# The second MLP's contraction by seven products of quarters, with products added onto each other in PSUM

## The chip, the core and the metric

The kernel runs on one core of a Trainium2 chip. The metric is the device time of one execution in microseconds; the time given is the median of three runs. One more execution was profiled, and all rows come from that one.

## What is computed

Three parts run one after the other on 4 x 576 = 2,304 tokens with 512 features: attention with a banded mask, an MLP with a product gate, and an MLP with a Silu gate. The change lies in the last one, cut here to what matters:

```python
# x: (2304, 512), from attention and the first MLP
g = x @ w_gate                        # (2304, 1536)
silu = g * (1.0 / (1.0 + np.exp(-g)))
val = x @ w_val                       # (2304, 1536)
out = (silu * val) @ w_out            # (2304, 512)
```

## The kernel before

**Precision.** Every fp32 operand is split into two parts of the type fp32r, a rounded one (ScalarE, a copy) and the rest (VectorE, a subtraction): `to_parts`, lines 163 to 165. A product of two operands is three matmuls, `mm3`, lines 222 to 224. Its time appears at these three lines whatever is multiplied, so the names of the tiles tell the parts of the kernel apart.

**Stage 1** has attention and the first MLP, in chunks of 512 tokens and a last one of 256. For each of 8 groups of features, the gates `ba` (copied by ScalarE, line 241, to `ta`) and `bb` (multiplied by VectorE, line 247) are made, and the result is contracted. Beside it `quarters` prepares the weights of stage 2, one step at a time (`step`, called after each group; `work` is the list of steps): a block of 1 MB is loaded into one of two `raw` buffers, turned to fp32 (line 205 on ScalarE, 206 and 207 on VectorE), for the gate and value weights summed (lines 535 to 538), split by `split_to` (line 518 on ScalarE, 519 on GpSimd) and stored to the DRAM tensors `wd` and `wod` (line 556). `QUARTERS` says how many of the 18 blocks each chunk takes.

**Stage 2** runs over 3 column blocks `c` of 768 tokens and in each over 6 groups `j` of 256 features: 18 groups. The gate and the value of a group are each made by seven products of quarters (two halves of the 512 inputs, of the 256 features, of the 768 tokens), with sums and differences of quarters, in place of eight. `operands` makes the seven token-side sums once for a column block (line 629, split at 164 and 165); the weight-side ones come from `wd` through a ring of 14 places (`fill`, line 653), each of which holds the gate's and the value's part for one product. `product` makes product `r` for the gate and then for the value: 12 matmuls of 384 columns, each in its own PSUM bank of a set of three. `evacuate` reads the banks: a ScalarE copy for the first product (line 713), VectorE sums for the rest (line 704), Silu on ScalarE (707), the multiplication on VectorE (708), and the split of the result to `p`.

The contraction of a group with `w_out` is then plain: six units (`units`), one for 128 tokens, each 6 matmuls of 512 columns into one of two banks, and an addition to `acc` by VectorE (line 746; line 744 is a copy for the first group). Units go to the list `todo`, and `contract_some` takes one after each of the first six products of the next group. After the last group the remaining six run on their own. `load_wo` (line 760) loads two tiles of weights for a group, into four buffers.

The queues of the engines are filled by a scheduler that works on a model of the times, so an instruction of a later group may stand ahead of one of an earlier.

Of the kernel before, what the change touches and what calls it, by code (L numbers as in the profile page):

```python
# [10 lines left out]
F32 = mybir.dt.float32  # L11
# [65 lines left out]
S1, S2, S4, S3, A11, A12, A22 = range(7)  # L77
SPOT = [A11, S2, A12, S1, S3, S4, A22]

BANK = [0, 1, 2, 0, 1, 2, 0]  # L80

NOP = 9
NRING = 14

UNITS = [1, 1, 1, 1, 1, 1, 0]
# [4 lines left out]
def moe_chain_kernel(tc, q_in, k_in, v_in, w_in, mask_in, out):  # L90
# [8 lines left out]
    with static as st, other as ot, psum as pp, dram as dp:  # L99
# [16 lines left out]
        wd = dp.tile([FP, P, 7, 2, 2, 2 * P], F32R, name="wd")  # L116
        wod = dp.tile([FP, P, 2, 2 * 512], F32R, name="wod")
# [101 lines left out]
        def mm3(ps, w, x, start, stop):  # L219

            (wh, wl), (xh, xl) = w, x
            nc.tensor.matmul(ps, wh, xh, start=start, stop=False)  # L222
            nc.tensor.matmul(ps, wh, xl, start=False, stop=False)  # L223
            nc.tensor.matmul(ps, wl, xh, start=False, stop=stop)  # L224
# [52 lines left out]
        with att1_pool as a1, att2_pool as a2:  # L277
# [243 lines left out]
            def quarters():  # L521
# [7 lines left out]
                if kind != "wo2":  # L529

                    b = x.rearrange("p i (j f) -> p i j f", j=2)
                    t = raw_at[n][:, :, :, 1].bitcast(F32).rearrange("p i (j f) -> p i j f", j=2)
                    t = {S1: t[:, 0, 0], S2: t[:, 0, 1], S4: t[:, 1, 0], S3: t[:, 1, 1]}
                    add = nc.vector.tensor_tensor
                    add(out=t[S1], in0=b[:, 1, 0], in1=b[:, 1, 1], op=ALU.add)
                    add(out=t[S3], in0=b[:, 0, 0], in1=b[:, 1, 0], op=ALU.subtract)
                    add(out=t[S2], in0=t[S1], in1=b[:, 0, 0], op=ALU.subtract)
                    add(out=t[S4], in0=b[:, 0, 1], in1=t[S2], op=ALU.subtract)
                    yield
                for i in range(2):  # L540
                    stage = stages[n_stage[0] % 2]
                    n_stage[0] += 1
                    if kind == "wo2":
                        w = stage[:, :1024].rearrange("p (b h f) -> p b h f", b=1, h=2)
                        split_to(w, x[:, i:i + 1])
                        dst, src = wod[j, :, i], stage[:, :1024]
                    else:
                        w = stage.rearrange("p (s h f) -> p s h f", s=7, h=2)
                        m = ("wg", "wv").index(kind)
                        f = slice(i * P, (i + 1) * P)  # L550
# [45 lines left out]
        with mid_pool as mp:  # L596
# [19 lines left out]
            def operand(c, r):  # L616
                return ops[(7 * c + r) % NOP]
# [234 lines left out]
```

## Time and profile before

| | us |
|---|---|
| median of 3 runs (lowest, highest) | 877.03 (876.01, 877.11) |
| the profiled execution | 877.38 |
| its span | 875.6 |
| TensorE busy | 848.3 (97%) |
| VectorE busy | 563.3 (64%) |
| ScalarE busy | 347.4 (40%) |
| GpSimd busy | 110.3 (13%) |

In the rows PE is TensorE's matmuls, PEld its weight loads, DVE VectorE, ACT ScalarE, POOL GpSimd, SP SyncE, and a q behind an engine its queue. `out<-in` names tiles by the program's names. Matmuls overlap and their ends are modelled, so the time of one is read from the start of one to the start of the next. A busy time is the time in which at least one instruction ran.

### The profile page before, as it was taken

What the parts mean: (1) busy time and instruction counts of PE and PEld (TensorE: products, weight loads), DVE (VectorE), ACT (ScalarE), POOL (GpSimd) and SP (SyncE); (2) the same over time, 40 slices, a digit from 0 to 9 for tenths busy, and PEclk for the clock granted to TensorE, in tenths of its full rate; (3) what the DMA queues carried; (4) which work ended last, traced back from release to release, by engine and by line L of the source; (5) the groups of instructions that cost most, each with busy time, mean ns of one, the idle gap of its engine ahead of it and who ended that gap; (6) DMA issues with size and microseconds to landing.
All of it is one profiled execution on the core that took longest, in us unless ns stands there. A gap on an engine that the chain in (4) does not pass through costs nothing.

```text
span 875.6 us, 12949 instructions
## 1 busy us (share of the span) xinstructions
PE 848.3 (97%) x4846; PEld 744.6 (85%) x4846; DVE 563.3 (64%) x989; ACT 347.4 (40%) x819; POOL 110.3 (13%) x120
## 2 busy tenths in 40 slices
PE   7889999999999999999799999999999999999998
PEld 5668788888887777787799999999999999999997
DVE  6899964275437452363468766797666686666676
ACT  5687755375536453343344222242222232222221
POOL 1000144035304440153210000000000000000000
PEclk9889999999999999999899999999999999999999
DMA  9997558269625762785899666587766667766311
GB/s 294 345 286 260 179 167 277 53 189 318 215 69 172 255 186 84 235 267 189 267 360 389 204 210 214 179 285 233 244 201 197 205 215 258 226 214 215 122 49 72
DMA packets 79279, 188.20 MB, mean 215 GB/s; under 512 B 6896, under 2 KB 42352, under 8 KB 74480
## 3 DMA queue, kind: packets, MB, share of 16 engines
q1 hardware_dynamic: 76336, 182.65, 64.5%
q10 hardware_dynamic: 2880, 4.72, 1.5%
q8 instruction: 38, 0.62, 0.3%
q14 instruction: 25, 0.20, 0.1%
HBM read 148.29 MB, written 39.06 MB: 214 GB/s over the span
## 4 chain that ended last, share of the span: by engine, by line
PE 53%; DMA 7%; DVE 2%; issue 2%; POOL 1%; ACT 1%; SPq 0%; ACTq 0%; POOLq 0%; DVEq 0%
PE bk L222 18%; PE bk L224 18%; PE bk L223 17%; DMA raw<-w_in 5%; POOL mid L519 1%; DMA wd<-mid 1%; DMA x1d<-o 1%; DMA wd<-stage 1%; DVE raw L207 1%; DMA raw<-x1d 0%; POOL stage L519 0%; ACT mid L518 0%; ACT s L346 0%; DVE p L165 0%; PE bk L379 0%
## 5 line engine op out<-in xcount | busy, mean ns | idle before, releaser
L704 DVE TENSOR_TENSOR s<-bk,s 128x384 f32<-128x384 f32 x252 | 137.7, 554 | 64.8 <-ACT s L713 38.1
L222 PE MATMUL bk<-x,w 128*128 128x512 f32 (+2 forms) x368 | 136.4, 372 | 6.5 <-ACT ta L241 6.5
L223 PE MATMUL bk<-x,w 128*128 128x512 f32 (+2 forms) x368 | 135.8, 369 | 1.5 <-DVE x L165 1.5
L224 PE MATMUL bk<-x,w 128*128 128x512 f32 (+2 forms) x368 | 135.7, 369 | 0.0
L707 ACT ACTIVATE s<-s 128x384 f32<-128x384 f32 x72 | 37.8, 525 | 147.3 <-DVE s L704 147.2
L222 PEld LDWEIGHTS bk<-x,w 128*128 128x128 f32 x368 | 70.2, 191 | 17.8 <-ACT ta L241 8.3
L222 PE MATMUL bk<-wo,p 128*128 128x512 f32 x216 | 85.2, 394 | 0.0
L223 PE MATMUL bk<-wo,p 128*128 128x512 f32 x216 | 84.7, 392 | 0.0
L224 PE MATMUL bk<-wo,p 128*128 128x512 f32 x216 | 82.6, 394 | 0.0
L223 PEld LDWEIGHTS bk<-x,w 128*128 128x128 f32 x368 | 70.2, 191 | 11.9 <-DVE x L165 1.9
L224 PEld LDWEIGHTS bk<-x,w 128*128 128x128 f32 x368 | 70.1, 191 | 9.8
L746 DVE TENSOR_TENSOR acc<-bk,acc 128x512 f32<-128x512 f32 x90 | 61.9, 688 | 24.0 <-PE bk L224 23.5
L164 ACT ACTIVATE p<-s 128x384 fp32r<-128x384 f32 x72 | 37.8, 525 | 84.9 <-DVE s L708 84.9
L222 PE MATMUL bk<-w 128*128 128x384 f32 (+1 forms) x196 | 70.8, 367 | 0.2 <-ACT w L200 0.2
L223 PE MATMUL bk<-w 128*128 128x384 f32 (+1 forms) x196 | 70.4, 362 | 0.4 <-DVE w L201 0.4
L223 PE MATMUL bk<-w,mid 128*128 128x384 f32 x204 | 68.7, 337 | 0.0
L222 PE MATMUL bk<-w,mid 128*128 128x384 f32 x204 | 68.7, 337 | 0.0
L224 PE MATMUL bk<-w,mid 128*128 128x384 f32 x204 | 68.5, 337 | 0.0
L224 PE MATMUL bk<-w 128*128 128x384 f32 (+1 forms) x196 | 67.5, 357 | 0.0
L247 DVE TENSOR_TENSOR ta<-bk,ta 128x512 f32<-128x512 f32 (+1 forms) x40 | 25.3, 633 | 62.6 <-ACT ta L241 31.4
L224 PE MATMUL bk<-p,W 128*128 128x512 f32 (+1 forms) x160 | 60.2, 378 | 0.0
L519 POOL TENSOR_TENSOR stage<-raw,stage 128x512 fp32r<-128x512 f32 (+2 forms) x54 | 53.1, 1007 | 52.0 <-ACT stage L518 52.0
(103 smaller groups left out, 1661.0 us busy)
## 6 DMA issues: line engine op xcount, KB each, us to landing
mid<-wd SPq DMA_DIRECT2D x72, 512.0 KB, 4.5
raw<-w_in SPq DMA_DIRECT2D x31, 1024.0 KB, 8.1
w<-wd SPq DMA_DIRECT2D x45, 512.0 KB, 3.8
wo<-wod SPq DMA_DIRECT2D x36, 512.0 KB, 5.5
wd<-stage SPq DMA_DIRECT2D x16, 896.0 KB, 6.5
wd<-mid SPq DMA_DIRECT2D x8, 896.0 KB, 5.4
v<-v_in SPq DMA_DIRECT2D x16, 432.0 KB, 6.8
early<-w_in SPq DMA_DIRECT2D x6, 1024.0 KB, 12.3
```

The lines of the kernel that those rows point to most:

```text
L164: nc.scalar.activation(hi, src, AF.Copy)
L207: nc.vector.scalar_tensor_tensor(out=lo, in0=hi, scalar=3, in1=lo, op0=ALU.logical_shift_left, op1=ALU.bitwise_or)
L222: nc.tensor.matmul(ps, wh, xh, start=start, stop=False)
L223: nc.tensor.matmul(ps, wh, xl, start=False, stop=False)
L224: nc.tensor.matmul(ps, wl, xh, start=False, stop=stop)
L247: nc.vector.tensor_tensor(out=u, in0=bb[:, :n], in1=ta[:, :n], op=ALU.mult)
L519: nc.gpsimd.tensor_tensor(out=dst[:, :, 1], in0=src, in1=dst[:, :, 0].bitcast(F32), op=ALU.subtract)
L704: nc.vector.tensor_tensor(out=dst[m], in0=x[m], in1=y[m], op=ALU.add)
L707: nc.scalar.activation(u[0], u[0], AF.Silu)
L746: nc.vector.tensor_tensor(out=a, in0=ps, in1=a, op=ALU.add)
```

## The change

Four things change, all for stage 2.

1. The contraction takes two groups of features at a time (256 + 256) and is made by seven products of quarters too: `units(q)` for each of 9 pairs. Quarters are halves of the pair's features, of the 512 results and of the 768 tokens. The results stand with their features on the partitions, so the output is stored transposed. A unit is one of 7 products for one of two 128-feature halves of the results: 6 matmuls of 384 columns. One unit follows every second product. `sums` makes the operands from the gated values `u`, in place, 768 columns at a time.
2. Products that go into one result with the same sign are added onto each other in PSUM, with no VectorE sum: `product` writes product `i` to bank X, Z or Y by `XZXYXZX`, and S2, S3, S4 and A22 are added onto what stands there. Where the value in between is needed, ScalarE copies it to a temporary tile first (`copy`), and the next product on that bank has to wait for the copy. All seven products of the gate now come ahead of the seven of the value.
3. The contraction's weights `w_out` get their sums in `quarters` as the others do, so all blocks have the same steps, and `wod` holds seven parts.
4. Buffers: the ring has 9 places in place of 14, the operands of the contraction 4 (`NPO`), its weights 4 (`NWO`). `operands` makes its differences in place.

```diff
-                if kind != "wo2":
...
+                t1, t2, t3, t4 = t[:, 0, 0], t[:, 0, 1], t[:, 1, 0], t[:, 1, 1]
+                add = nc.vector.tensor_tensor
+                add(out=t1, in0=b[:, 1, 0], in1=b[:, 1, 1], op=ALU.add)
+                add(out=t3, in0=b[:, 0, 0], in1=b[:, 1, 0], op=ALU.subtract)
+                add(out=t2, in0=t1, in1=b[:, 0, 0], op=ALU.subtract)
+                add(out=t4, in0=b[:, 0, 1], in1=t2, op=ALU.subtract)
+                yield
                 for i in range(2):
...
+                    for g in range(2):
+                        split_to(w[:, S1 + 3 * g:S2 + 3 * g + 1], t[:, g, :, f])
+                    split_to(w[:, A11:A12 + 1:A12 - A11], b[:, 0, :, f])
+                    split_to(w[:, A22:A22 + 1], b[:, 1, 1:2, f])
...
+            def less(dst, in0, in1):
+                nc.vector.tensor_tensor(out=dst, in0=in0, in1=in1, op=ALU.subtract)
+                return dst
+
+            def sums(b, order):
+
+                (b11, b12), (b21, b22) = b
+                of = {
+                    A11: lambda: b11, S1: lambda: less(b11, b12, b11), S2: lambda: less(b11, b22, b11),
+                    A12: lambda: b21, S3: lambda: less(b12, b22, b12), S4: lambda: b22,
+                    A22: lambda: less(b11, b21, b11),
+                }
+                return [of[r] for r in order]
...
-                fill({5: 10, 6: 12, 7: NRING}.get(k, 9 if k > 2 else 4))
+                fill({5: NRING - 5, 6: NRING - 3, 7: NRING}.get(k, NRING - 5 if k > 2 else 2))
...
+            def product(n, m, i):
+                c, j = divmod(n, FP)
+                if i == 0:
+                    x, z, y, v = chain["next"] if "next" in chain else pbank
+                    chain.update(X=x, Z=z, Y=y, next=[v, y, z, x])
+                ps = chain["XZXYXZX"[i]][:, :HT]
+                w, x = ring[n_used[0] // 2 % len(ring)][:, n_used[0] % 2], operand(c, i)
+                for kt in range(2):
+                    mm3(ps, (w[:, kt, 0], w[:, kt, 1]), (x[:, 0, kt], x[:, 1, kt]), i in (0, 1, 3) and kt == 0, kt == 1, i not in (0, 1, 3))
                 n_used[0] += 1
+                evacuate(n, m, i, ps)
+
+            def copy(src):
+                t = temp()
+                nc.scalar.activation(t, src, AF.Copy)
+                return t
+
+            def evacuate(n, m, i, ps):
+
+                def kept(k, in0=None, in1=None):
+                    g = gq[:, k]
+                    dst = uq[n // 2 % 2][:, k, n % 2] if m else g
+                    if in0 is not None:
+                        nc.vector.tensor_tensor(out=dst, in0=in0, in1=in1, op=ALU.add)
+                    src = ps if in0 is None else dst
+                    if m:
+                        nc.vector.tensor_tensor(out=dst, in0=src, in1=g, op=ALU.mult)
+                    else:
+                        nc.scalar.activation(dst, src, AF.Silu)
+
+                if i == A11:
+                    chain["a"] = copy(ps)
+                elif i == S1:
+                    chain["b"] = copy(ps)
+                elif i == S2:
+                    chain["d"] = copy(ps)
+                elif i == A12:
+                    kept(0, ps, chain["a"])
+                elif i == S3:
+                    kept(3, copy(ps), chain["b"])
+                elif i == S4:
+                    kept(1, ps, chain["d"])
+                else:
+                    kept(2)
...
+            def units(q):
...
+                def make():
+                    if made:
+                        r, of = made.popleft()
+                        o = late[0][(NPROD * q + r) % NPO]
+                        to_parts(of(), o[:, 0], o[:, 1])
+
+                def keep(ps, k, m, new, end):
+                    g, h = divmod(k, 2)
+                    a = oacc[:, 2 * g + m, h * HT:(h + 1) * HT]
+                    if new and first:
+                        nc.scalar.activation(a, ps, AF.Copy)
+                    else:
+                        nc.vector.tensor_tensor(out=a, in0=ps, in1=a, op=ALU.add)
+                    if end and last:
+                        t = c * TOK + h * HT
+                        nc.sync.dma_start(out=out[(2 * g + m) * P:(2 * g + m + 1) * P, t:t + HT], in_=a)
+
+                for r in range(2):
+                    make()
+                for r, s in enumerate(C_ORDER):
                     for m in range(2):
+                        def unit(r=r, s=s, m=m):
+                            t = NPROD * q + r
+                            w, x = late[1][t % NWO], late[0][t % NPO]
+                            ps = cbank[m][s in (S1, S4, A12)][:, :HT]
+                            for j in range(2):
+                                mm3(ps, (w[:, j, m, 0], w[:, j, m, 1]), (x[:, 0, j], x[:, 1, j]), s in (A11, S1, A12) and j == 0, j == 1, s not in (A11, S1, A12))
...
+                            keep(ps, k, m, new, end)
+                            if m == 1:
+                                load_wo(t + NWO)
                             else:
+                                make()
...
+                for m in range(2):
+                    for i in range(NPROD):
+                        product(n, m, i)
...
+                        fill()
+                        if (NPROD * m + i) % 2:
+                            contract_some(1)
+                        if m:
+                            step()
+                if n % 2:
+                    units(n // 2)
```

## Rows read from the trace of the kernel before

**Rows 1.** Windows: stretch and length, busy us of each engine, clock, DMA, GB/s.
```profile
400.00:430.00 30.00, 24.74 (x133) 21.14 (x132) 12.35 (x22) 11.74 (x24) 7.34 (x10) 0.93 0.62 213
...
461.00:871.90 410.90, 410.89 (x2148) 381.82 (x2147) 296.97 (x526) 104.07 (x194) 0.00 (x0) 1.00 0.63 207
```

**Rows 2.** TensorE's waits from 100 to 460 us: total us, times, longest.
```profile
PE bk L222 <- ACT ta L241: 6.5, 4, 4.7
```

**Rows 3.** Timeline of stage 2: start, duration, engine, line, operation, shapes.
```profile
501.27 0.39 PE L222 MATMUL bk<-wo,p 128*128 128x512 f32 x1
...
501.52 0.49 ACT L713 ACTIVATE s<-bk 128x384 f32<-128x384 f32 x1 [0.55 <-PE bk L224]
...
502.65 0.34 PE L222 MATMUL bk<-w,mid 128*128 128x384 f32 x1
...
504.74 0.40 PE L222 MATMUL bk<-wo,p 128*128 128x512 f32 x1
```

**Rows 4.** Timeline of TensorE's weight loads in stage 1, matmuls of 256 columns.
```profile
435.06 0.19 PEld L223 LDWEIGHTS bk<-x,w 128*128 128x128 f32 x1
...
435.18 0.19 PEld L224 LDWEIGHTS bk<-x,w 128*128 128x128 f32 x1
```

**Rows 5.** Groups by shape on VectorE: count, busy us, mean ns, idle before.
```profile
L704 DVE TENSOR_TENSOR s<-bk,s 128x384 f32<-128x384 f32 x252 | 137.7, 554 | 64.8 <-ACT s L713 38.1 <-PE bk L224 24.8
L746 DVE TENSOR_TENSOR acc<-bk,acc 128x512 f32<-128x512 f32 x90 | 61.9, 688 | 24.0 <-PE bk L224 23.5
L708 DVE TENSOR_TENSOR s<-s,s 128x384 f32<-128x384 f32 x72 | 40.1, 556 | 6.0
...
L165 DVE TENSOR_TENSOR w<-tx,w 128x768 fp32r<-128x768 f32 x9 | 8.6, 954 | 1.8 <-ACT w L164 1.8
...
L538 DVE TENSOR_TENSOR raw<-raw 128x256 f32<-128x256 f32 x12 | 6.5, 546 | 0.2
```

**Rows 6.** Groups by shape on ScalarE.
```profile
L707 ACT ACTIVATE s<-s 128x384 f32<-128x384 f32 x72 | 37.8, 525 | 147.3 <-DVE s L704 147.2
...
L713 ACT ACTIVATE s<-bk 128x384 f32<-128x384 f32 x36 | 17.7, 492 | 53.2 <-PE bk L224 53.2
...
L518 ACT ACTIVATE stage<-raw 128x512 fp32r<-128x512 f32 x22 | 13.9, 662 | 24.6 <-DMA wd<-stage 13.9 <-DVE raw L538 6.0 <-DVE raw L207 2.5
...
L164 ACT ACTIVATE w<-tx 128x768 fp32r<-128x768 f32 x9 | 7.6, 846 | 9.7 <-PE bk L224 7.5 <-DVE tx L629 2.2
...
L518 ACT ACTIVATE stage<-raw 128x256 fp32r<-128x256 f32 x16 | 6.9, 430 | 12.2 <-DMA wd<-stage 7.8 <-DVE raw L207 4.4
...
L518 ACT ACTIVATE stage<-raw 128x128 fp32r<-128x128 f32 x16 | 4.9, 308 | 0.0
```

**Rows 7.** DMA issues of stage 2 (count, size, landing), and a full window.
```profile
wo<-wod SPq DMA_DIRECT2D x36, 512.0 KB, 5.5
...
457.00:461.00 4.00, 4.00 (x32) 4.00 (x31) 2.35 (x5) 1.27 (x3) 0.00 (x0) 1.00 1.03 406
```

**Rows 8.** Groups by shape on GpSimd, stage 1.
```profile
L519 POOL TENSOR_TENSOR stage<-raw,stage 128x512 fp32r<-128x512 f32 x22 | 30.8, 1413 | 26.0 <-ACT stage L518 25.9
...
L519 POOL TENSOR_TENSOR stage<-raw,stage 128x256 fp32r<-128x256 f32 x16 | 13.2, 824 | 26.0 <-ACT stage L518 26.0
...
L519 POOL TENSOR_TENSOR stage<-raw,stage 128x128 fp32r<-128x128 f32 x16 | 10.1, 631 | 0.0
```

**Rows 9.** Timelines of SyncE and ScalarE around the gap.
```profile
415.78 1.41 SPq L155 DMA_DIRECT2D raw<-w_in  x1
...
425.29 1.10 ACT L205 ACTIVATE raw<-raw 128x1024 f32<-128x1024 f32 x1 [7.12 <-DMA raw<-w_in]
...
427.34 0.37 ACT L241 ACTIVATE ta<-bk 128x256 f32<-128x256 f32 x1
```

**Rows 10.** Timelines of TensorE and VectorE at the end.
```profile
863.37 0.39 PE L222 MATMUL bk<-wo,p 128*128 128x512 f32 x1
...
871.93 0.69 DVE L746 TENSOR_TENSOR acc<-bk,acc 128x512 f32<-128x512 f32 x1 [0.67 <-PE bk L224]
```

More of the change, by code (lines that the diff above doesn't have):

```diff
@@ L75 @@
 NC2 = NT // TOK
-S1, S2, S4, S3, A11, A12, A22 = range(7)
-SPOT = [A11, S2, A12, S1, S3, S4, A22]
-BANK = [0, 1, 2, 0, 1, 2, 0]
+NPROD = 7
+A11, S1, S2, A12, S3, S4, A22 = range(NPROD)
+C_ORDER = [A11, S1, S2, S4, S3, A12, A22]
 NOP = 9
-NRING = 14
-UNITS = [1, 1, 1, 1, 1, 1, 0]
+NRING = 9
+NPO = 4
+NWO = 4
 QUARTERS = [3, 4, 4, 5, 2]
@@ L680, in moe_chain_kernel @@
+                wo_ = [lp.tile([P, 2, 2, 2, P], F32R, name=f"wo{i}") for i in range(NWO)]
+                a_ = lp.tile([P, KT, TOK], F32, name="acc")
+                return po, wo_, a_
+            pbank = batt + [ba, bb]
+            cbank = [[acc[0], acc[1]], [acc[2], acc[3]]]
             late = []
             todo = deque()
-            n_unit = [0]
-            def product(c, j, r):
-                w, x = ring[n_used[0] % len(ring)], operand(c, r)
-                for m in range(2):
-                    ps = banks[m][BANK[r]][:, :HT]
-                    for kt in range(2):
-                        mm3(ps, (w[:, m, kt, 0], w[:, m, kt, 1]), (x[:, 0, kt], x[:, 1, kt]), kt == 0, kt == 1)
-                n_used[0] += 1
@@ L732, in units @@
[L732 to L749 removed]
+            chain = {}
@@ L755, in contract_some @@
                     n -= 1
-            def load_wo(n):
-                if n < FP * NC2:
-                    for i in range(2):
-                        nc.sync.dma_start(out=late[1][n % 2 * 2 + i].rearrange("p h f -> p (h f)").bitcast(F32), in_=wod[n % FP, :, i].bitcast(F32))
             for n in range(FP * NC2):
@@ L766, in moe_chain_kernel @@
                     step(2)
[L767 to L782 removed]
+                for m in range(2):
+                    for i in range(NPROD):
+                        product(n, m, i)
+                        if n == m == 0 and i == 2:
+                            flush_first()
+                            late.extend(start_late())
+                            for t in range(NWO):
+                                load_wo(t)
+                        fill()
[5 more added lines that the diff above has]
+                    units(n // 2)
             contract_some(99)
```

182 lines of the change are left out of this document (58 added, 124 removed).

## The prediction

> **What bounds the kernel now.** I read the busy times by stretch first, then TensorE's waits, then the timeline of TensorE, then the groups by shape, and last the stretches around the start and the end of stage 2. From 461 us on TensorE is busy for 410.89 of 410.90 us, VectorE for 297, ScalarE for 104, at full clock and with the DMA engines at 0.63 [rows 1]. The reader is to see that nothing but TensorE sets the pace there. Ahead of it there is one gap, between 400 and 430 us, with a granted clock of 0.93 [rows 1]; the list of TensorE's waits has 6.5 us on one ScalarE copy, 4.7 of them at once, and no wait after 461 us [rows 2]. So in stage 2 only fewer or shorter matmuls can help, and any new wait of TensorE costs its full length.
>
> **TensorE's work.** Before, the 18 groups have 6 contraction units each, of 6 matmuls with 512 columns. The timeline shows a unit from 501.27 to 502.65, 1.38 us, so 0.230 us a matmul; the 12 matmuls of 384 columns that follow take until 504.74, 2.09 us, so 0.174 each [rows 3]. 108 units x 1.38 = 149.0 us. After, two groups share 14 units of 6 matmuls with 384 columns: 9 x 14 x 6 = 756 x 0.174 = 131.5 us. The 1,512 matmuls of the products stay at 384 columns. The difference is 17.5 us, and it is columns only: 7/8 of them are left, although there are 756 instructions where there were 648.
>
> A weight load shows 0.19 us and so is longer than the 0.174 us between matmuls. But in stage 1 loads of 0.19 us start 0.12 us apart, one for each matmul of 256 columns [rows 4], so they overlap each other and aren't the limit at 0.174. I take 0.174.
>
> The Trainium skill (Perfetto Trace Analysis, "Identifying the Most-Contended Engine") says that TensorE's headroom is judged by the share of time in which weights are loaded, not by its matmul time. By that rule the loads would be the limit, more matmuls would cost more, and the kernel would get slower, as the last rival below. The starts in [rows 4] speak against it.
>
> **VectorE, for two groups.** Before: 28 sums of products x 0.554, 12 additions to the result x 0.688, 8 multiplications and 8 splits x about 0.555: 15.5 + 8.3 + 8.9 = 32.7 us [rows 5] in 2 x (14.6 + 8.3) = 45.8 us of TensorE. After: 12 sums and 8 multiplications (11.1), 14 additions of 384 columns (7.8 at 0.554), 7 splits and 4 differences of 768 columns (11 x 0.954 = 10.5): 29.4 us in 43.8 us. It has less to do, and stays off the path.
>
> **ScalarE, for two groups.** Before 4 copies x 0.492, 8 Silu and 8 splits x 0.525: 10.4 us. After 16 copies (7.9), 8 Silu (4.2), 7 splits of 768 columns x 0.846 (5.9): 18.0 us, and 6.9 more in the pairs that start a result, of 43.8 us [rows 6]. There is room, but now TensorE depends on it: in each chain of 7 products three are added onto a bank that ScalarE has yet to copy (S2 onto A11, S3 onto S2, A22 onto S3), 3 x 36 = 108 places. The copy's own path is short: TensorE leaves the product at 501.27, the copy starts at 501.52 and takes 0.49 [rows 3], so the bank is free 0.74 us after. Between two products of one bank lies another product (1.04 us) and, from the third group on, one unit (1.04 us): the slack is 1.34 us, and 0.30 us in the first two groups. Ahead of a copy in the queue there can be a Silu (0.525) that waits for VectorE's sum (0.554), or a split (0.846) that waits for a difference (0.954). One of them fits into 1.34 us, two don't. The bounds are 0 and, with one in three late by 0.25 us, 9 us. I take 1.5 us, nearest to nothing, because before ScalarE's copies start as soon as their bank is there and it is idle more than half of the time after as well.
>
> **The DMA queue.** For two groups 14 transfers of weights stay, and 7 of the contraction's take the place of 4, 512 KB each: 21 x 0.52 MB in 43.8 us is 252 GB/s where 207 were moved at a share of 0.63 [rows 1]; in proportion 0.77. The contraction's weights land after 5.5 us [rows 7]; with 4 buffers, each used for 2 units of a steady 6.3 us, they have over 15 us. The ring falls from 14 places to 9, which is 18 products and 9 units, 28 us ahead. In the first groups DMA is full (share 1.03 at 457 to 461 us [rows 7]); there a place lasts 2.09 us, 250 GB/s against the 406 seen. I cost all of it at nothing; without the cover of the ring each late place would stop TensorE for the rest of its landing time.
>
> **The conversion of the weights in stage 1.** A block of the contraction's weights now gets VectorE's 4 sums (4 x 0.53 [rows 5]) and 1,792 columns to split instead of 1,024. On GpSimd that is 2 x (3 x 0.82 + 0.63) = 6.2 us in place of 2 x 1.41, on ScalarE 2 x (3 x 0.43 + 0.31) = 3.2 in place of 1.3 [rows 6, 8]; a block of the other weights gets one instruction more per half. Over 18 blocks: GpSimd 26 us, ScalarE 16, VectorE 13, over some 320 us in which all have idle time; hidden by TensorE's own work in most places. The exception is the one gap. There the load of the last block was issued at 415.78, behind the stores of a block before it; ScalarE reached its first instruction on it (line 205) and stood until 425.29; the gate's copy (line 241), for which TensorE waited, is behind it at 427.34 [rows 9]. A block has now 4 steps where some had 3, so the block whose end frees the buffer comes later by up to one of its steps (about 4 us), and the last block's GpSimd work ends another 3.4 us later, and with it comes the load of the second half of stage 2's inputs. The instructions may also fall so that the gate's copy comes ahead of the load's wait. Bounds: -4.7 us (the gap is gone) and +7.5 us (4 + 3.4, all passed on). I take +2.
>
> **The end.** Before, the last product is followed by 6 units, from 863.37, and the last VectorE addition starts at 871.93 [rows 10]; TensorE didn't stop. After, 1 unit of the pair before and 14 units of the last pair are left: 15 x 1.04 = 15.6 us, already in the sum. VectorE has in this time 10 instructions of 768 columns (9.5 us), 15 additions (8.3) and one multiplication (0.6), 18.4 us, and ScalarE's split stands between a difference and its rest. So VectorE sets the end: +2.5 us, between 0 (busy times overlap a little) and 5 (the splits of three more differences, 0.85 each, exposed).
>
> **Sum.** The profiled execution took 877.38 us, span 875.6 and 1.8 around it; the median of the three runs is 877.03, so it stands for them. -17.5 + 1.5 + 2 + 2.5 = -11.5: 865.5 from the median. Likeliest case: 859 to 872.
>
> **Rivals.**
> *Late copies (slower).* Where three quarters of the 108 dependent products find their bank still being read, each late by 0.3 us, it costs 24 us: 877 - 17.5 + 4.5 + 24 = 888. It decides from 0.12 us on average over the 108 (13 us), which needs copies that start over 1.4 us late. For it: ScalarE's queue is in order, as the copy behind line 205 shows [rows 9]. Against it: the share of 0.4 to 0.55 and the slack of 1.34 us. Chance 0.08.
> The Trainium skill (Perfetto Trace Analysis, "Matmuls") advises to rotate independent groups of matmuls through different banks, so that a bank is emptied under the next group; here two products of one bank have only one other product and a unit between them. By it the waits are to be expected; no row of before shows such a bank.
> *A longer gap.* If the last block's load and the inputs behind it pass on the full 7.5 us and the copies and the end cost half of their upper bounds (7 us), 877 - 17.5 + 14.5 = 874, and up to 878. Against it: TensorE has products to fill with. Chance 0.10.
> *The gap closes.* The order around 415 us comes out otherwise, and the copies cost nothing: 877 - 17.5 - 4.7 + 1 = 856. Chance 0.12.
> *Loads of weights are the limit.* With 1,512 + 756 loads one behind the other at 0.19 us, stage 2 takes 431 us against the 411 of now: 877 + 20 = 897. The starts in stage 1 [rows 4] speak against it; it is also how the change would not do what it says, fewer columns for no time. Chance 0.02.
> The likeliest case has the rest, 0.68.
>
> **How the numbers follow.** Faster and slower begin at 0.2%, 1.8 us, about what the runs of this kernel can tell from no change. Faster: 0.68 + 0.12 + half of the longer gap = 0.85. The same: 0.05, the other half. Slower: 0.10, late copies and loads. The range goes from 856, where the gap closes, to 877, and leaves out the two slow cases and the end of the longer gap.
>
> **What would show it.** Contraction matmuls of 384 columns 0.174 us apart, and a stage 2 of about 394 us of matmuls: right. A list of TensorE's waits with the copies of the product banks at more than 5 us in sum: the first price was wrong. A wait of over 9 us on line 241's copy: the gap. From the last product to the last addition over 21 us: the end. VectorE busy in more than 0.8 of a stretch, or a wait on the ring: I missed a bound.

## The result, and the profile after

The changed kernel takes **857.02 us** (median of 4 runs, 855.5 to 858.1) against 877.07 us (4 runs, 876.01 to 877.7) for the kernel before in the same comparison: ratio 0.9771, 95% interval 0.9751 to 0.9792. It is faster by 20.05 us, where 11.5 were predicted: inside the range, 8.5 us below the predicted time, and 1 us from the rival in which the gap closes (856). The profiled execution took 856.14 us, span 854.4.

Windows of the changed kernel; columns as in [rows 1].

```profile
300.00:400.00 100.00, 98.91 (x547) 80.72 (x546) 44.14 (x77) 40.87 (x101) 32.69 (x44) 1.00 0.58 182
400.00:430.00 30.00, 25.10 (x153) 21.58 (x152) 15.84 (x26) 15.05 (x36) 15.49 (x22) 1.00 0.86 292
430.00:460.00 30.00, 30.00 (x233) 30.00 (x232) 17.25 (x30) 16.41 (x35) 5.66 (x8) 1.00 0.95 323
...
600.00:700.00 100.00, 100.00 (x576) 100.00 (x575) 60.06 (x97) 44.27 (x83) 0.00 (x0) 1.00 0.80 266
...
800.00:840.00 40.00, 37.06 (x212) 36.42 (x210) 23.85 (x41) 14.23 (x25) 0.00 (x0) 1.00 0.43 131
840.00:854.40 14.40, 10.87 (x60) 10.29 (x60) 9.19 (x15) 0.96 (x2) 0.00 (x0) 1.00 0.53 178
```

In stage 2 TensorE is still the only full engine: 576 matmuls in 100 us, all of 384 columns, 0.1736 us each. VectorE has fallen from the 0.72 of [rows 1] (296.97 of 410.9) to 0.60, ScalarE has risen from 0.25 to 0.44, the DMA share from 0.63 to 0.80. The last two windows hold what is new: TensorE stands still near the end, as it did not before. The stretch from 400 to 430 us has about the busy time of before (25.10 for 24.74), but the clock in it is now 1.00 where it was 0.93.

TensorE's waits of the changed kernel from 380 to 460 us, and from 460 us to the end (both lists whole): total, times, longest.

```profile
PE bk L221 <- ACT ta L240: 3.1, 4, 1.1
PE bk L221 <- ACT p L163: 1.8, 1, 1.8
PE bk L222 <- DVE p L164: 0.2, 1, 0.2
...
PE bk L221 <- ACT po L163: 1.7, 1, 1.7
PE bk L222 <- DVE po L164: 1.4, 1, 1.4
```

Lines 221 to 223 are the three matmuls, 163 and 164 the splits, 240 the gate's copy (241 before). No wait in stage 2 is on a product bank's copy (line 710); the two that there are belong to the operands `po` of the last contraction. The single wait of 4.7 us on the gate's copy [rows 2] has become several of about 1 us and one of 1.8 us on the split. In sum they are not shorter; the whole list of the kernel before from 380 to 460 us is

```profile
PE bk L222 <- ACT ta L241: 5.2, 2, 4.7
```

So TensorE waits there for 5.1 us where it waited for 5.2, in shorter pieces and with the clock at 1.00 all through.

Timeline of the changed kernel on SyncE and ScalarE where the gap was; it answers to [rows 9].

```profile
417.33 0.50 SPq L154 DMA_DIRECT2D raw<-w_in  x1
...
422.65 0.36 ACT L240 ACTIVATE ta<-bk 128x256 f32<-128x256 f32 x1
...
426.38 1.17 ACT L204 ACTIVATE raw<-raw 128x1024 f32<-128x1024 f32 x1 [1.76 <-DMA raw<-w_in]
427.42 0.39 ACT L240 ACTIVATE ta<-bk 128x256 f32<-128x256 f32 x1
```

The load is issued 1.55 us later than before, and ScalarE still waits for it. But one gate's copy (422.65) now stands ahead of that wait in ScalarE's queue, and the wait has shrunk from 7.12 to 1.76 us.

**Where the time came from.** Each group leaves a mark on ScalarE: before, the copy of its first product (line 713) at 500.48 and 15 groups later at 845.18, 22.98 us a group; after, the Silu that reads the bank of the gate's last product (line 724) at 497.84 and 14 groups later at 804.44, 21.90 us a group. 18 x 1.08 = 19.4 us. The waits at the end give 3.1 back: 16.3 us from stage 2. The rest, 20.05 - 16.3 = 3.7 us by the medians, comes from ahead of it. In the two profiles the last gate's copy of stage 1 starts at 456.37 before and at 450.83 after, 5.5 us apart; the difference up to the 29th of these 40 copies (384.69 and 382.05) is 2.6 us, so 2.9 of it fall into the stretch with the gap. The 3.7 is a difference of medians of 4 runs; how firm it is, the section on the prediction asks.

### The profile page after: what moved, and what is told of

Its sections match the earlier page's. It is cut to its first block, busy times and chain, and to the rows that moved or that the text cites. A ratio compares the mean times of both kernels' runs of the same rounds, so it can differ in the third digit from the quotient of the medians.

```text
span 854.4 us, 13410 instructions
## 1 busy us (share of the span) xinstructions
PE 827.0 (97%) x4954; PEld 751.8 (88%) x4954; DVE 527.4 (62%) x890; ACT 427.0 (50%) x1002; POOL 131.6 (15%) x180
## 4 chain that ended last, share of the span: by engine, by line
PE 76%; DMA 12%; DVE 6%; ACT 3%; POOL 2%; issue 1%; SPq 1%; ACTq 0%; DVEq 0%; POOLq 0%
PE bk L221 23%; PE bk L222 23%; PE bk L223 23%; DMA raw<-w_in 4%; DMA early<-w_in 3%; PE bk L326 3%; POOL u L518 2%; DMA wd<-u 2%; PE bk L378 2%; DMA wod<-u 2%; PE bk L363 1%; DMA k<-k_in 1%; DVE raw L206 1%; DVE w L200 1%; ACT s L345 1%
## 5 line engine op out<-in xcount | busy, mean ns | idle before, releaser
L221 PE MATMUL bk<-x,w 128*128 128x512 f32 (+2 forms) x400 | 146.6, 367 | 3.9 <-ACT ta L240 3.9
L223 PE MATMUL bk<-x,w 128*128 128x512 f32 (+2 forms) x400 | 146.4, 366 | 0.0
L222 PE MATMUL bk<-x,w 128*128 128x512 f32 (+2 forms) x400 | 146.0, 365 | 0.1
L221 PE MATMUL bk<-w 128*128 128x384 f32 (+1 forms) x264 | 93.2, 359 | 0.2 <-ACT w L199 0.2
L222 PE MATMUL bk<-w 128*128 128x384 f32 (+1 forms) x264 | 92.5, 352 | 0.5 <-DVE w L200 0.5
L223 PE MATMUL bk<-w 128*128 128x384 f32 (+1 forms) x264 | 89.4, 350 | 0.0
L222 PE MATMUL bk<-po,wo 128*128 128x384 f32 x252 | 84.4, 336 | 1.4 <-DVE po L164 1.4
L221 PE MATMUL bk<-po,wo 128*128 128x384 f32 x252 | 83.5, 336 | 1.7 <-ACT po L163 1.7
L223 PE MATMUL bk<-po,wo 128*128 128x384 f32 x252 | 84.6, 336 | 0.0
L768 DVE TENSOR_TENSOR acc<-bk,acc 128x384 f32<-128x384 f32 x102 | 55.8, 553 | 46.2 <-PE bk L223 46.0
L518 POOL TENSOR_TENSOR stage<-raw,stage 128x256 fp32r<-128x256 f32 x88 | 63.9, 754 | 59.0 <-ACT stage L517 59.0
L163 ACT ACTIVATE po<-u 128x768 fp32r<-128x768 f32 x63 | 52.5, 843 | 31.3 <-PE bk L223 15.3
L710 ACT ACTIVATE u<-bk 128x384 f32<-128x384 f32 x80 | 38.8, 490 | 56.7 <-PE bk L223 55.6
L164 DVE TENSOR_TENSOR po<-u,po 128x768 fp32r<-128x768 f32 x63 | 59.6, 952 | 8.9 <-ACT po L163 8.8
L204 ACT ACTIVATE raw<-raw 128x1024 f32<-128x1024 f32 (+1 forms) x33 | 37.4, 1133 | 49.7 <-DMA raw<-w_in 49.7
L222 PE MATMUL bk<-p,W 128*128 128x512 f32 (+1 forms) x160 | 58.9, 373 | 0.2 <-DVE p L164 0.2
L223 PE MATMUL bk<-p,W 128*128 128x512 f32 (+1 forms) x160 | 58.9, 372 | 0.0
L221 PE MATMUL bk<-p,W 128*128 128x512 f32 (+1 forms) x160 | 57.1, 376 | 1.8 <-ACT p L163 1.8
```

The costliest lines, as they stand in the source:

```text
L163: nc.scalar.activation(hi, src, AF.Copy)
L164: return nc.vector.tensor_tensor(out=lo, in0=src, in1=hi.bitcast(F32), op=ALU.subtract)
L204: nc.scalar.activation(hi.bitcast(F32), hi.bitcast(F32), AF.Prelu, scale=REBIAS, alpha=SIGN_UP)
L221: nc.tensor.matmul(ps, wh, xh, start=start, stop=False, skip_group_check=onto)
L222: nc.tensor.matmul(ps, wh, xl, start=False, stop=False, skip_group_check=onto)
L223: nc.tensor.matmul(ps, wl, xh, start=False, stop=stop, skip_group_check=onto)
```

## The experiments

Each was timed beside the kernel before (medians of 876.1 to 876.6 us). "After" is the changed kernel, 857.02.

### The columns alone: an eighth product

```diff
-                            for j in range(2):
+                            for j in (0, 1, 0, 1) if s == A11 else (0, 1):
```

> The changed kernel, whose contraction does its first product (A11) twice for each unit, the second time over the first, so that it has as many columns as before (8 products of 384 in place of 6 units of 512 for each of two groups). Theory (the columns of the contraction are the gain in stage 2): 9 x 2 x 6 matmuls x 0.174 = 18.8 us more than the changed kernel, so about 876, and within 0.5% of the kernel before only because some 5 us gained ahead of stage 2 are lost to the end. Rival (fewer sums for VectorE, and products added in PSUM, are worth a part): the added matmuls fill time in which TensorE would wait or run beside something else, and it stays under 870.

Measured: 873.66 us (871.36 to 876.2, 10 runs), ratio 0.997 (0.9953 to 0.9987); 16.6 us above after. 9 pairs x 12 matmuls x 0.1736 = 18.7 us are added. TensorE's waits from 440 us on, in this kernel:

```profile
PE bk L221 <- DVE acc L768: 0.8, 1, 0.8
```

The two waits at the end (3.1 us) have gone, since the longer units cover them, and 0.8 came: 18.7 - 3.1 + 0.8 = 16.4, as measured. The profiles say the same without medians: from the last gate's copy of stage 1 to the end of the span it takes 419.2 us before, 403.5 in after and 419.8 here. So the eighth of the contraction's columns is the gain of stage 2. All other edits together are worth 3 us by the medians (876.64 - 873.66).

### ScalarE's copies two and three times

The second kernel has `range(3)`.

```diff
-                nc.scalar.activation(t, src, AF.Copy)
+                for _ in range(2):
+                    nc.scalar.activation(t, src, AF.Copy)
```

> The changed kernel with each ScalarE copy of a product bank made twice, one right behind the other, into the same tile: 16 copies more for two groups (7.9 us of ScalarE). Theory (the copies end 0.74 us after their product, the slack is 1.34 us): 0.4 us more fit into the slack from the third group on; only the first two groups, with 0.30 us, can lose, 12 places x 0.1 to 0.2 = 1 to 2 us. So 857 to 860. Rival (TensorE already waits on late copies, in waits too short to see): 108 places x up to 0.4 us, over 880.

> The changed kernel with each ScalarE copy of a product bank made three times. Theory: the bank is free 0.74 + 2 x 0.41 = 1.56 us after its product, past the slack of 1.34, and ScalarE is busy for 34 of 44 us in two groups: 108 places x 0.2 us = 22 us, and more where a split stands ahead: 875 to 895. If it stays within 5 us of the changed kernel, the slack is larger than I worked out (the scheduler puts more work between two products of a bank).

Measured: twice 860.11 us (856.28 to 861.5, 4), ratio 0.9808 (0.9767 to 0.9849); three times 868.47 us (866.03 to 872.67, 6), ratio 0.9914 (0.9886 to 0.9943). TensorE's waits from 440 us on with two copies (the whole list), and then the largest with three:

```profile
PE bk L221 <- ACT po L163: 1.6, 1, 1.6
PE bk L221 <- ACT u L711: 1.1, 1, 1.1
PE bk L222 <- DVE po L164: 0.7, 2, 0.4
```

```profile
PE bk L221 <- ACT po L163: 3.3, 5, 1.3
PE bk L221 <- ACT u L711: 2.8, 3, 1.0
```

A window of steady stage 2 with three copies:

```profile
500.00:600.00 100.00, 98.68 (x563) 97.39 (x562) 68.33 (x108) 72.87 (x151) 0.00 (x0) 1.00 0.77 258
```

With twice the copies, 0.49 us more on every path from a bank to the next product on it, one product in 108 was late, by 1.1 us. Three copies, 0.98 us more, gave waits on three copies of `u` and one of `ta` (0.3 us, in the same list), 3.1 us in sum. From the first Silu of the second group to the last Silu of stage 2 they cost 6.7 us (363.52 for 356.85), where two cost 0.3 (357.16). Not all of the 6.7 stands in the list of waits; where the rest goes isn't shown. So late copies were far from deciding. The second expectation missed: 11.5 us by the medians, where it had at least 18. Copies that run late in one place aren't late everywhere.

### The conversion of the contraction's weights

The first kernel is the one before with the weights converted in seven parts, as after does it. The second is after with the plain split: the weights get no sums, and the contraction reads four parts in place of seven.

```diff
-                if kind != "wo2":
+                if kind == "wo2":
+                    b = x.rearrange("p j (i f) -> p i j f", i=2)
+                else:
                     b = x.rearrange("p i (j f) -> p i j f", j=2)
...
+                    for g in range(2):
+                        split_to(w[:, 2 * g:2 * g + 2], tt[:, g, :, f])
```

```diff
+                if kind != "wo2":
...
+                    if kind == "wo2":
+                        split_to(stage[:, :1024].rearrange("p (b h f) -> p b h f", b=1, h=2), x[:, i:i + 1])
...
-                    src = wod[q % (FP // 2), :, C_ORDER[r]].rearrange("p j i f -> p (j i f)")
+                    src = wod[q % (FP // 2), :, C_ORDER[r] % 4].rearrange("p j i f -> p (j i f)")
```

> The kernel before, whose blocks of the contraction's weights get the four sums and are split and stored in seven parts as in the changed kernel; the contraction reads two of these parts in place of the plain halves, so its result is not the reference's. All else is as before. Theory A (what was gained ahead of stage 2 came from the other order of the conversion's steps, which puts the gate's copy ahead of the load that ScalarE stood on): 3 to 6 us faster than before, 871 to 874, and no wait of over 2 us on the gate's copy. Theory B (as I predicted: more conversion work makes the gap longer): 2 to 8 us slower, and what was gained came from the ring or the products instead.

> The changed kernel with the contraction's weights split plainly in stage 1, as before (no sums, two splits of 512 columns for a block, 3 steps); the contraction reads four stored parts in place of seven, so its result is not the reference's. Stage 2 is untouched. Theory (about 2 us of what was gained ahead of stage 2 come from the conversion's new steps, by way of the gap's clock): the gap of over 4 us on the gate's copy is back, 859 to 862. Rival (less conversion work is only less work): 853 to 856, some 2 us faster, and the conversion was a cost.

Measured: before with the conversion 875.75 us (874.4 to 876.7, 10), ratio 0.999 (0.9976 to 1.0004); after without it 856.64 us (856.12 to 857.14, 4), ratio 0.9777 (0.9764 to 0.9789). Neither time moved. The window of before with the conversion, its largest wait from 380 to 460 us, and ScalarE's timeline where the gap was:

```profile
400.00:430.00 30.00, 25.31 (x141) 21.31 (x140) 14.50 (x25) 13.69 (x35) 14.98 (x23) 1.00 0.90 293
```

```profile
PE bk L222 <- ACT ta L241: 4.6, 5, 1.5
```

```profile
427.36 0.36 ACT L241 ACTIVATE ta<-bk 128x256 f32<-128x256 f32 x1
427.62 1.40 ACT L518 ACTIVATE mid<-raw 128x256 fp32r<-128x256 f32 x4
428.92 0.41 ACT L164 ACTIVATE p<-ta 128x256 fp32r<-128x256 f32 x1
430.91 1.18 ACT L205 ACTIVATE raw<-raw 128x1024 f32<-128x1024 f32 x1 [1.58 <-DMA raw<-w_in]
```

The gate's copy stands ahead of the load's wait here too, as it does in after: the conversion alone moved ScalarE's queue. The traces show more than that. Compared by line and shape, ScalarE's first 670 instructions, TensorE's first 2,602, VectorE's first 468 and all 180 of GpSimd stand in the order in which they stand in after; the first that differs in after starts at 440 us. So the half of Theory A on the wait came true (no wait of over 2 us, clock 1.00), and the half on the time did not: the order of after, up to 440 us, brought 0.9 us here (by the interval, between a loss of 0.4 and a gain of 2.1).

The same for after without it, whose only wait there is 1.7 us on the gate's copy:

```profile
400.00:430.00 30.00, 28.32 (x173) 25.35 (x172) 15.62 (x24) 13.19 (x30) 11.59 (x16) 1.00 0.67 224
```

The first has cut the long wait into five without getting the time back. The second has almost no wait left, although in it the load's wait stands ahead of the gate's copy as in the kernel before (ScalarE's timeline):

```profile
421.71 1.13 ACT L204 ACTIVATE raw<-raw 128x1024 f32<-128x1024 f32 x1 [4.05 <-DMA raw<-w_in]
...
423.80 0.36 ACT L240 ACTIVATE ta<-bk 128x256 f32<-128x256 f32 x1
```

From the 29th to the last gate's copy it takes 64.74 us, against 68.78 in after and 71.68 before. Six of the kernels of this section (the eighth product, the copies, the end) have the instructions of after in the same order on all engines up to 440 us, and this stretch takes 65.9 to 68.3 us in them. So the price of the conversion in it is between 1 and 4 us. The 29th copy comes 3.9 us later than in after; in those six it comes up to 4.5 us later with the very same instructions. What this profile wins in the stretch, the medians don't show.

### The ring of 9 in the kernel before, and both together

```diff
-NRING = 14
+NRING = 9
...
-                fill({5: 10, 6: 12, 7: NRING}.get(k, 9 if k > 2 else 4))
+                fill({5: NRING - 5, 6: NRING - 3, 7: NRING}.get(k, NRING - 5 if k > 2 else 2))
```

> The kernel before with the ring of 9 places and the filling order of the changed kernel, and the stages in tiles of their own. Theory (the ring is no cause): within 1 us of before, 876 to 878, with the gap of 4.7 us as it was. Rival (fewer early transfers into the ring let the last block's load land earlier, and that closes the gap): 2 to 4 us faster, 873 to 875, with the last block's load landing in under 8 us.

> The kernel before with both: the contraction's weights converted in seven parts (the result is not the reference's) and the ring of 9 places with its filling order. All that the change does ahead of stage 2, with the products and the contraction as before. Theory (the gain ahead of stage 2 is conversion and ring, and not the products): 872 to 874, 3 to 4 us faster than before. Rival (it is the new order of the products, which leave the gates' banks and the matmul queue at the end of stage 1 alone): as with the conversion alone, 875 to 877.

Measured: the ring 883.49 us (880.17 to 886.74, 6), ratio 1.0086 (1.0066 to 1.0106); with the conversion as well 875.52 us (870.62 to 879.11, 12), ratio 0.9994 (0.9978 to 1.001). The window at the start of stage 2 of the kernel before with the ring of 9; TensorE's only wait from 430 us on is one of 2.0 us on VectorE's sum of products (line 704).

```profile
460.00:500.00 40.00, 37.97 (x201) 36.05 (x200) 29.55 (x55) 11.31 (x22) 0.00 (x0) 0.96 0.76 262
```

7 us lost, with TensorE short of 2 us in the first 40 of stage 2. So a smaller ring brings no gain; in the old order it costs something (4.2 us between the two profiles), with the filling order and the places of the stages moved beside it. Why that is gone again with the conversion wasn't found. The kernel with both has the order of after on all four engines up to 440 us as well, and in the list of DMA issues up to 449 us: up to there it is the stage 1 of after, and it gained 0.6 us.

### The gap alone: the order of ScalarE's queue

In the kernel before, what ScalarE does for the blocks of weights in the first two groups of the last chunk is queued behind ScalarE's half of the latest split of gated values (`last_a`), and so behind that group's gate copy.

```diff
-                        with tc.issue_after(last_p[0]):
-                            next(work[0])
+                        with tc.issue_after(last_p[0]):
+                            if pin:
+                                with tc.issue_after(last_a[0]):
+                                    next(work[0])
...
-                step(99 if k == K1 - 1 else 4 if k < 2 else 2)
+                step(99 if k == K1 - 1 else 4 if k < 2 else 2, pin=k < 2)
```

> The kernel before, with ScalarE's part of the conversion in the first two groups of the last chunk queued behind the gate's split, so that line 205's wait for the last block no longer stands ahead of the gate's copy (line 241). ScalarE's queue is the same as before up to there. Theory (what was gained ahead of stage 2 is the gap: 4.7 us of waiting and some 2 us at a clock of 0.59 and 0.73): 3 to 5 us faster, 871 to 874, with a clock of 1.00 from 400 to 460 us. Rival (the gap hides other waits, as the conversion alone showed, which had no gap and gained 0.9 us): within 1.5 us of before, since the inputs of stage 2 come later by as much and TensorE waits for them.

Measured: 870.75 us (868.91 to 872.81, 6), ratio 0.9934 (0.9918 to 0.9951): 5.8 us faster than the kernel before. The window, and ScalarE's timeline in it (lines 243, 166 and 207 are 241, 164 and 205 of before):

```profile
400.00:430.00 30.00, 28.78 (x170) 25.13 (x169) 16.29 (x25) 13.69 (x28) 11.69 (x13) 1.00 0.73 249
```

```profile
422.99 0.37 ACT L243 ACTIVATE ta<-bk 128x256 f32<-128x256 f32 x1
...
427.11 0.42 ACT L166 ACTIVATE p<-ta 128x256 fp32r<-128x256 f32 x1
427.43 1.15 ACT L207 ACTIVATE raw<-raw 128x1024 f32<-128x1024 f32 x1
```

The gate's copy and the split stand ahead of the instruction on the loaded block, which finds its data there when its turn comes. The stretch from the 29th to the last gate's copy takes 66.04 us for 71.68: 5.6 us less. Its 29th copy comes 1.6 us later than before, so the profile as a whole is 4.6 us shorter, where the medians say 5.8. The longest wait from 400 to 460 us is 0.9. So the gap of before is worth some 5 to 6 us, more than its 4.7 us of waiting; what the clock adds is told at the end. This isn't the queue of after, where the instruction on the load still waits for 1.76 us, ahead of the next gate's copy.

The same in the changed kernel, with the last group of the chunk before pinned too:

> The changed kernel with ScalarE's part of the conversion queued behind the gate's split, in the last group of the chunk of 512 tokens before the last and in the first two groups of the last chunk (the same edit as in the kernel before, one group more). Theory (the conversion's instructions ahead of the gate's copy and split are what TensorE waits for at the end of stage 1, and the time lost there isn't lost elsewhere): the waits of 1.8, 0.8 and 0.9 us between 415 and 428 us go away, 3 us faster than the changed kernel, 853.5 to 855, below both kernels. Rival (the inputs of stage 2 come later and TensorE waits for them): 856 to 858, with a wait after 440 us.

Measured: 860.52 us (858.31 to 863.19, 5), ratio 0.982 (0.9797 to 0.9843); not faster. ScalarE's timeline at the place, then TensorE's, then two windows:

```profile
433.22 0.96 ACT L520 ACTIVATE u<-raw 128x256 fp32r<-128x256 f32 x3 [2.63 <-DMA wd<-u]
434.09 0.40 ACT L165 ACTIVATE p<-ta 128x256 fp32r<-128x256 f32 x1
```

```profile
434.54 0.74 PE L223 MATMUL bk<-p,W 128*128 128x256 f32 x4 [1.30 <-ACT p L165]
```

```profile
430.00:435.00 5.00, 3.60 (x27) 3.39 (x28) 3.78 (x8) 2.19 (x7) 1.26 (x2) 1.00 1.03 314
435.00:440.00 5.00, 4.76 (x28) 4.56 (x27) 1.50 (x3) 2.28 (x7) 4.25 (x7) 0.66 1.02 346
```

Another wait took the place of the one removed: three conversions stand ahead of the split of `p` in ScalarE's queue, and wait for stores of the block before. TensorE stood for 1.4 of 5 us, and in the next 5 the clock was 0.66. The stretch takes 68.76 us, as in after (68.78), at the upper end of what it takes without the pin (65.9 to 68.8), so the pin gained nothing there. This profile is 4.3 us longer than that of after, and 4.4 us of lag were there at the 29th copy already, ahead of what was pinned.

### The end: less for VectorE, other buffers, no differences

Three kernels edit the last pair of groups alone. The first gives GpSimd one of VectorE's four differences and two of its rests.

```diff
-                    A12: lambda: b21, S3: lambda: less(b12, b22, b12), S4: lambda: b22,
+                    A12: lambda: b21, S3: lambda: less(b12, b22, b12, eng), S4: lambda: b22,
...
+                        if q == FP // 2 * NC2 - 1 and C_ORDER[r] in (S4, A12):
+                            src = of()
+                            nc.scalar.activation(o[:, 0], src, AF.Copy)
+                            nc.gpsimd.tensor_tensor(out=o[:, 1], in0=src, in1=o[:, 0].bitcast(F32), op=ALU.subtract)
```

> The changed kernel; for the last pair of groups alone GpSimd, which is idle in stage 2, makes the difference S3 and the rests of the operands S4 and A12 in VectorE's place. Theory (VectorE sets the end, with 18 us of work for 15.6 us of matmuls): VectorE loses 2.9 us of work, TensorE's two waits of 1.4 and 1.7 us after the last product shrink to under 1.5 us in sum, and the time falls by 1.5 to 2.5 us, to 854.5 to 855.5. Rival (the chain difference, split, rest sets the end, or GpSimd slows VectorE): no change or 1 us slower.

The second puts the last three operands into buffers that are free by then, so that no split waits for a unit to have read its buffer.

```diff
-                        o = late[0][(NPROD * q + r) % NPO]
+                        o = late[0][(NPROD * q + r) % NPO] if q < q_last or r < NPO else operand(NC2, r - NPO)
```

> The changed kernel; the last three operands of the last pair go into buffers of the token operands, which have no user any more, in place of the four that turn. VectorE's work is the same. Theory (VectorE's work sets the end): no change of the sum of TensorE's waits (3.1 us), or under 1 us. Rival (the buffers set it): the second wait, 1.7 us on ScalarE's split, goes away, 855.3.

The third leaves the four differences out.

```diff
+                if q == FP // 2 * NC2 - 1:
+                    made = deque((r, lambda k=k: u[:, k]) for r, k in enumerate((0, 1, 3, 3, 1, 2, 2)))
```

> The changed kernel; in the last pair of groups the four differences are left out and the operands are made from the gated values as they are, so the result is not the reference's. VectorE has 3.8 us less to do after the last product, and no operand depends on another. Theory (VectorE's work sets the end): TensorE's waits of 3.1 us at the end fall below 1 us, 854 to 855. Rival (the buffers set it: a split waits until the units of four operands earlier are done): a wait of 1.5 us or more on ScalarE's split stays.

| | median us (runs) | ratio | waits at the end | last Silu to the end of the span |
|---|---|---|---|---|
| after | 857.02 (855.5 to 858.1) | 0.9771 | 3.1 | 826.75 to 854.4: 27.65 |
| GpSimd helps | 860.13 (855.41 to 863.03) | 0.9809 | 3.6 | 825.17 to 853.6: 28.43 |
| other buffers | 860.71 (854.46 to 862.39) | 0.9802 | 3.3 | 824.49 to 852.7: 28.21 |
| no differences | 855.52 (849.11 to 857.3) | 0.9744 | 0 | 829.05 to 852.8: 23.75 |

The last Silu is a fixed point of the program ahead of these edits. It starts 4.6 us apart in the four profiles, though the instructions of stage 1 stand in the same order on all engines up to 440 us. Medians that lie 3 us apart are thus not a reading of the end; the last column is. By it, GpSimd's help and the other buffers brought nothing, and leaving out the differences 3.9 us. The timeline of after at the end, VectorE's rows and then TensorE's:

```profile
834.61 0.95 DVE L627 TENSOR_TENSOR u<-u 128x768 f32<-128x768 f32 x1
835.47 0.95 DVE L164 TENSOR_TENSOR po<-u,po 128x768 fp32r<-128x768 f32 x1
```

```profile
836.48 0.44 PE L222 MATMUL bk<-po,wo 128*128 128x384 f32 x1 [1.44 <-DVE po L164]
...
840.17 0.79 PE L221 MATMUL bk<-po,wo 128*128 128x384 f32 x3 [1.67 <-ACT po L163]
```

The timeline of the kernel where GpSimd helps, VectorE and then GpSimd:

```profile
833.03 1.94 DVE L164 TENSOR_TENSOR po<-u,po 128x768 fp32r<-128x768 f32 x1
...
835.36 2.12 DVE L627 TENSOR_TENSOR u<-u 128x768 f32<-128x768 f32 x1
...
839.21 2.63 DVE L164 TENSOR_TENSOR po<-u,po 128x768 fp32r<-128x768 f32 x1
```

```profile
834.11 2.55 POOL L763 TENSOR_TENSOR po<-u,po 128x768 fp32r<-128x768 f32 x1
...
839.17 1.85 POOL L763 TENSOR_TENSOR po<-u,po 128x768 fp32r<-128x768 f32 x1 [2.51 <-ACT po L762]
```

In after, the rest that TensorE waits for (835.47) stands behind a difference (834.61, line 627) on a VectorE that is busy nearly without a pause from 829.6 to 843.2. GpSimd took three instructions away, and three of those that were left took 1.94, 2.12 and 2.63 us in place of 0.95: what was saved was lost again.

## Why the prediction held, and where its size was off

**The columns: right.** 17.5 us were predicted; 19.4 were measured by the periods, and the eighth product adds 18.7 us of matmuls back. The sum took matmuls of 384 columns as 0.174 us apart, and in after they are 0.1736. What was predicted from two units of one timeline (22.9 us a group of before, 21.9 after) is 22.98 and 21.90 by the marks; the difference of the rounded values was 0.1 us a group too small. With the eighth product done again, 16.6 us of the time came back, less than 18.7 because the waits at the end went away.

**Weight loads as the limit: refuted.** The loads are at 100.00 of 100 us and TensorE still starts a matmul every 0.1736 us, with loads of 0.19 us. The reading of [rows 4], that loads overlap each other, held. The Trainium skill (Perfetto Trace Analysis, "Identifying the Most-Contended Engine") has TensorE's headroom judged by the share of its peak rate that the matmuls use and by the busy share of weight loads. The second did not give the time here: that share went from 0.93 to 1.00, and the matmuls kept their pace.

**The copies: price too high.** 1.5 us were put in; no wait on a product's bank shows, so the term is 0. With the copies doubled one wait showed in 108 places: the path has about 0.49 us to spare nearly everywhere. The Trainium skill (Perfetto Trace Analysis, "Matmuls") advises that independent groups of matmuls rotate through different banks; here a product and a unit lay between two products of one bank, and the trace shows no wait.

**The ring, the DMA queue, VectorE's and ScalarE's loads: right in the main.** 0.77 of DMA, 29.4 of 43.8 us of VectorE (0.67) and 18.0 of ScalarE (0.41) were worked out for steady stage 2; from 600 to 700 us they are 0.80, 0.60 and 0.44, and TensorE waits for none of them. That 9 places do for the new order doesn't carry over: in the old order they cost 7 us. One figure was too high: in a pair that starts a result ScalarE makes 8 copies into it (24 in the trace for three such pairs), 3.9 us and not 6.9, since the other 6 of 14 are additions on VectorE.

**The end: size right, in part by luck.** TensorE waits for 3.1 us there, where 2.5 were put in. From the last product (833.49) to the end of the last addition (851.64) it takes 18.15 us; the prediction had 15.6 + 2.5 = 18.1, but its 15 units are 13 in the trace (78 matmuls, 13.5 us), with 4.6 us on top of them in place of 2.5, so the agreement of the sum is luck. It put the end on VectorE's work of 18.4 us. The four differences of that work set it: without them there is no wait, and the end is 3.9 us shorter. Whether their place in the chain of difference, split and rest does it, or the 3.8 us that they take, was not separated: without them both are gone. The buffers of the operands are ruled out.

**The step that failed: "the conversion of the weights in stage 1".** It was put at +2 us, with the gap living on or growing. The long wait went away. By the medians what lies ahead of stage 2 gained 3.7 us, so the term was wrong by 5.7, and with the copies (1.5) and the columns (1.9) that makes up the 8.5 (the end took 0.6 back). The prediction named what happened as one of its bounds (the gate's copy comes ahead of the load's wait) and gave it a chance of 0.12. Which edit moved the order is shown: the conversion, which by itself gives the kernel before the queues of after up to 440 us.

That the moved order brought the 3.7 us is not shown, and the runs speak against it: with the same order the kernel before gained 0.9 us, and 0.6 with the ring; and the changed kernel without that conversion, in which the load's wait stands ahead of the gate's copy again, is as fast (856.64 us). In after TensorE waits as long in sum as before (5.1 us for 5.2); what the stretch gained (2.9 us by the profiles) is about what the clock had cost in the kernel before (2.2 us, an estimate worked out at the end). Nor is the 3.7 firm. For each of the six other kernels with the order of after up to 440 us, take from its gain by the medians what its profile gains from the last gate's copy to the end: 0.7 to 3.6 us are left, where after itself leaves 4.4 (20.05 - 15.7). So conversion, ring and order together did not cost 2 us, as predicted, but gained between 0.6 and 4.4 in the kernels that have them; what brings the part above 1 us, if it is there, stays open. The order of ScalarE's queue can be worth more: in the kernel before, an order that left no wait on the load at all gained 5.8 us.

**No faster version.** Of the kernels that do the whole computation, none is faster than after by more than their runs scatter.

## What to carry to other kernels

Where one engine is full in a whole stage, fewer columns come out of the time one for one, and a handful of timeline rows prices them to a tenth; the error of the forecast then lies in the stages beside it. A queue that is worked off in order, with a wait for a transfer in it, should be read as a place whose order decides microseconds: look at what stands directly behind the waiting instruction, and test the order alone before crediting any edit with it. Compare the queues of two kernels instruction by instruction: it tells which edit moved an order, and which time differences are between executions of the same instructions. Price small changes by the distance between two marks in one profile that enclose the edit, not by medians of kernels whose other parts move by several microseconds; and read such a distance in several profiles, since the stretch above took 65.9 to 68.8 us with the same instructions.

## What was not expected of the hardware

**VectorE beside GpSimd.** A VectorE subtraction of 128x768 with both inputs in SBUF took 0.95 us alone and 1.94, 2.12 and 2.63 us beside GpSimd's instruction of the same shape. The Trainium skill (SBUF — State Buffer, "Who interferes with whom") states that a VectorE instruction with two SBUF inputs contends with a GpSimd instruction that reads SBUF, and that the shared pair of ports is an exclusive lock. The trace agrees in that VectorE's instructions took two to three times as long; it doesn't show which of the two had to wait.

**What the clock adds to a gap.** Two windows of the kernel before, around its 4.7 us wait:

```profile
425.00:430.00 5.00, 2.24 (x10) 2.24 (x11) 1.66 (x3) 3.67 (x9) 2.46 (x4) 0.59 0.56 215
430.00:435.00 5.00, 5.00 (x34) 5.00 (x33) 3.63 (x4) 1.60 (x4) 2.74 (x2) 0.73 0.62 206
```

After TensorE had stood, the granted clock was 0.59 and 0.73 in these stretches, near the lower of its two levels (1.2 for 2.4 GHz) and then on the way back: 34 matmuls in 5 us, where 44 fit from 435 to 440 us at 1.00. The ten that are missing there, at 5/44 us each, are 1.1 us on top of the wait; the ten of the stretch before took 2.24 us where they would take 1.1. Together that is an estimate of 2.2 us for the clock. The several waits of 1 us in after left the clock at 1.00.
